# Another order of the opening steps in a fused retention and feed-forward kernel, with less VectorE work on SBUF and the last output in the score banks

## The chip, the cores and the metric

The kernel runs on one NeuronCore of a Trainium2 chip. Times are device microseconds (us) of one execution. Medians come from unchanged repeats; the profile is one of the executions. "Span" is the time from the first to the last instruction in the profile; it is about 1.7 us shorter than the device time. The engines are called PE (TensorE), DVE (VectorE), ACT (ScalarE), POOL (GpSimd) and SP (the queue that issues most loads) in profile lines.

## The reference

```python
def _attn_ref(q, k, v):                      # 8 x 8 heads x 576 x 64
    scores = (1/sqrt(64)) * (q @ k^T)
    gamma  = 1 - 2 ** (-5 - arange(H))       # one per head
    Dmat   = where(i >= j, gamma ** (i - j), 0)
    return (scores * Dmat) @ v
x   = attention, as 4608 tokens x 512
out = ((x @ w_a) * (x @ w_b)) @ w_out        # w_a, w_b 512 x 1536, w_out 1536 x 512, float32
```

The kernel does the matmuls in bf16. It never forms `Dmat`: the decay is split into a factor on each value row (`vs`) and one on each output row (`qs`), and keys outside a 128-row block come in through a running state.

## The kernel before

The feed-forward (36 block rows of 128 tokens) keeps PE busy for most of the span. It can only start once the first 512 tokens of x exist. The opening makes these in four steps, each of 256 tokens (`n`) and four heads (`hh`). All q, k, v pieces of a step (256 KB each) are loaded, cast to bf16, transposed on PE, and go through scores, state and output:

```python
STEPS = [(0, 0), (1, 0), (0, 1), (1, 1)]            # (n, hh): order 0, 1, 2, 3
for i, which in ((0, Q), (0, K), (2, K), (2, Q), (1, Q), (0, V),
                 (1, K), (1, V), (3, K), (3, Q), (2, V), (3, V)):
    load_step(*STEPS[i], which)                     # on SP's queue
...
def output_step(i):
    o = ps_o[0].tile([128, 2, 512], FP32, tag="o", name="o0")      # one buffer
    ... # matmuls: state x q, then values x masked scores
    nc.vector.tensor_tensor(x_of(...), o, qs, op=ALU.mult)         # scaled, PSUM to SBUF
...
warm(8, 512)                # dummy matmuls while nothing has landed
for c in range(HP):
    make_qs(c, 0, 512)      # four tables of decay factors, on ScalarE
cast_step(0, Q, "dve"); cast_step(0, K, "dve")
transpose_step(0, Q, "dve"); ...; transpose_step(0, K, "act")      # copies out of PSUM
warm(4, 256); score_step(0)
...                         # steps 2, 1, 3 interleaved, with dummies
state_step(3, (0,))
for F in range(3):
    ffn_begin(F)            # six of the first twelve w_a matmuls
output_step(3)
warm(3, 256)
```

`warm(count, n)` issues dummy matmuls of n columns that keep PE active. Later in the kernel, in the second half of the first feed-forward block, tiles 4 and 5 (128 tokens each) are made on the side, and then pairs of tiles. The argument will touch these lines, which the change leaves alone:

```python
def cast(i, on="pool"):                    # tiles 4 and 5: on == "dve"
    nc.scalar.copy(qb, qf)                 # q on ScalarE
    if on == "dve":
        nc.vector.tensor_copy(kb, kf)      # k on VectorE, SBUF to SBUF
...
def state(i):                              # the last of these, i == 5
    for r in (0, 1):
        rows = slice(64 * r, 64 * r + 64)
        nc.vector.tensor_copy(sums[rows, 3], kv[rows, :, rows])
        nc.scalar.copy(into[rows, 0], kv[rows, :, rows])
...
def ahead(n):                              # pairs of tiles, n = 3 first
    for w, t in ((0, qf), (1, kf)):
        nc.gpsimd.tensor_copy(qkb[0:64, w], t[0:64])     # 64 x 1024 on GpSimd
```

Of the kernel before, what the change touches and what calls it, by code (L numbers as in the profile page):

```python
# [10 lines left out]
FP32 = mybir.dt.float32  # L11
# [3 lines left out]
ALU = mybir.AluOpType  # L15
# [3 lines left out]
def kernel(  # L19
# [10 lines left out]
    nc = tc.nc  # L30

    B, H, S, D = q.shape
# [5 lines left out]
    HP = H // 2  # L38
# [24 lines left out]
    const = pool("const", 1)  # L63
# [13 lines left out]
    ps_sc = pool("ps_sc", 1, PS)  # L77
    opening, ps_o = ExitStack(), {}
# [80 lines left out]

    STEPS = [(0, 0), (1, 0), (0, 1), (1, 1)]  # L160
    Q, K, V = 0, 1, 2
    for i, which in ((0, Q), (0, K), (2, K), (2, Q), (1, Q), (0, V),
                     (1, K), (1, V), (3, K), (3, Q), (2, V), (3, V)):
        load_step(*STEPS[i], which)


# [1 line left out]
    idxp_i = const.tile([128, 6], INT32)  # L168
# [20 lines left out]
    mask3 = const.tile([128, 64], BF16)  # L189

    def make_masks():
        nc.gpsimd.iota(idxv_i, pattern=[[256, BL], [128, 2]], base=0,
                       channel_multiplier=1)
        nc.gpsimd.memset(mask, 1.0)
        nc.gpsimd.affine_select(
            out=mask, in_=mask, compare_op=ALU.is_ge, fill=0.0,
            base=0, pattern=[[1, 128]], channel_multiplier=-1)
        nc.gpsimd.tensor_copy(mask2, mask)
        nc.gpsimd.memset(mask2[0:64, 64:128], 0.0)

    ones = const.tile([128, 512], BF16)
    nc.vector.memset(ones, 1.0)  # L202
    lgp = const.tile([128, HP], FP32)
    for c in range(HP):
        nc.vector.memset(lgp[0:64, c:c + 1], math.log(gammas[2 * c]))
        nc.vector.memset(lgp[64:128, c:c + 1], math.log(gammas[2 * c + 1]))
    biasq = const.tile([128, 1], FP32)
    nc.vector.memset(biasq, math.log(scale))
    idxp_f = const.tile([128, 6], FP32)
    nc.vector.tensor_copy(idxp_f, idxp_i)  # L210
    nc.vector.tensor_scalar_add(idxp_f[64:128, 4:5], idxp_f[64:128, 4:5],
                                -float(S))
    vs = const.tile([128, H, 6], FP32)
    for h in range(H):
        nc.scalar.activation(vs[:, h, :], idxp_f, AF.Exp,
# [7 lines left out]
    def make_qs(c, s0, s1):  # L223
        nc.scalar.activation(qs[:, c, s0:s1], idx_f[:, s0:s1], AF.Exp,  # L224
                             bias=biasq[:, 0:1], scale=lgp[:, c:c + 1])
# [32 lines left out]
                                 name="state2")  # L258
    states = [two_states[:, i] for i in (0, 1)]
    state_after = const.tile([128, 2, 2, HP, 128], BF16)  # L260
    for t in (state_after, two_states):
        nc.vector.memset(t, 0.0)

    def load_w(f0, f1, which="ab"):
        if "a" in which:
            nc.gpsimd.dma_start(wa_sb[:, :, f0:f1], wa_r[:, :, f0:f1])
        if "b" in which:
            nc.gpsimd.dma_start(wb_sb[:, :, f0:f1], wb_r[:, :, f0:f1])
# [34 lines left out]
    def given(i, which):  # L303
        n, hh = STEPS[i]
        return paired[n][which][:, hh * DM:(hh + 1) * DM].rearrange(
            "p (h k d) -> p h k d", h=4, k=2)

    def by_parity(t):
        return t.rearrange("p (k h d) -> p h k d", h=4, k=2)
# [4 lines left out]
    def cast_step(i, w, on):  # L314
        COPY[on](by_parity(natural[STEPS[i]][0][:, w]), given(i, w))

    def values_step(i, kp, on):
        n, hh = STEPS[i]
        on.tensor_tensor(
            by_parity(natural[n, hh][1])[:, :, kp], given(i, 2)[:, :, kp],  # L320
            vs[:, 4 * hh:4 * hh + 4, 2 * n + kp].unsqueeze(2)
            .to_broadcast([128, 4, D]), op=ALU.mult)

    def transpose_step(i, w, on):
        qkb, qkT = natural[STEPS[i]][0], transposed[STEPS[i]]
        tp = ps_ffn.tile([128, 4, 128], BF16, tag="ab", name="tp")
        for c in range(4):
            nc.tensor.transpose(tp[:, c, :], qkb[:, w, c * 128:c * 128 + 128],  # L328
                                identity)
        COPY[on](qkT[:, w], tp.rearrange("p c x -> p (c x)"))  # L330
# [26 lines left out]
    def state_step(i, behinds):  # L357

        n, hh = STEPS[i]
        kv = ps_ffn.tile([128, 2, 2, 64], FP32, tag="ab", name="kv0")  # L360
        fresh = {0, 1}
        for behind in behinds:
            parts = [(0, slice(0, 128))] if n else []
            parts.append((n, slice(0, 128) if behind else half(0)))
            for m, rows in parts:
                qkb, vb = natural[m, hh]
                for j in (0, 1):
                    for kp in (0, 1):
                        for r in (0, 1):
                            e0 = kp * 256 + (2 * j + r) * 64  # L370
                            nc.tensor.matmul(  # L371
                                kv[half(r), behind, j, :],
                                qkb[rows, 1, e0:e0 + 64],
                                vb[rows, e0:e0 + 64],
                                start=r in fresh, stop=True,
                                skip_group_check=True)
                            fresh.discard(r)
        which = slice(behinds[0], behinds[-1] + 1)
        for r in (0, 1):
            nc.scalar.copy(  # L380
                state_after[half(r), n, which, 2 * hh:2 * hh + 2, half(r)],
                kv[half(r), which])

    def output_step(i):
        n, hh = STEPS[i]
        vb = natural[n, hh][1]
        sT = scored.pop((n, hh))
        o = ps_o[0].tile([128, 2, 512], FP32, tag="o", name="o0")
        for a in (0, 1):
            if (n, a) == (0, 0):  # L390
                continue
            st = state_after[:, 0, 0] if (n, a) == (0, 1) else (
                state_after[:, n - 1 + a, 1 - a])
            for j in (0, 1):
                nc.tensor.matmul(o[:, a, 128 * j:128 * j + 128],
                                 st[:, 2 * hh + j, :],
                                 queries((n, hh), slice(0, 128), j, a),
                                 start=(j == 0), stop=True,
                                 skip_group_check=True)
        for j in (0, 1):  # L400
            for kp in (0, 1):
                for a, r in QUADS:
                    e0 = kp * 256 + (2 * j + r) * 64
                    nc.tensor.matmul(  # L404
                        o[half(r), a, 128 * j:128 * j + 128],
                        vb[half(a), e0:e0 + 64],
                        sT[half(a), r, j, kp],
                        start=((n, a, j, kp) == (0, 0, 0, 0)), stop=True,
                        skip_group_check=True)
        cs = slice(2 * hh, 2 * hh + 2)  # L410
        nc.vector.tensor_tensor(
            x_of(256 * n, 256)[:, cs].rearrange("p j (a s) -> p a j s", a=2),
            o[:, :, 0:256].rearrange("p a (j s) -> p a j s", j=2),
            qs[:, cs, 256 * n:256 * n + 256]
            .rearrange("p j (a s) -> p a j s", a=2), op=ALU.mult)
# [416 lines left out]
    def warm(count, n):  # L832

        w = ps_ffn.tile([128, 512], FP32, tag="ab", name="w")
        for _ in range(count):
            nc.tensor.matmul(w[:, 0:n], ones[:, 0:128], ones[:, 0:n],  # L836
                             start=True, stop=True)
# [1 line left out]
    W1, W2 = 128 * WCOLS[0], 128 * (WCOLS[0] + WCOLS[1])  # L839
    vector, pool_ = nc.vector, nc.gpsimd  # L840
    warm(8, 512)
    for c in range(HP):
        make_qs(c, 0, 512)
    for i in range(4):
        place_step(i)
    cast_step(0, Q, "dve")
    cast_step(0, K, "dve")
    transpose_step(0, Q, "dve")
    cast_step(2, K, "pool")
    transpose_step(0, K, "act")  # L850
    warm(4, 256)
    score_step(0)
    transpose_step(2, K, "act")
    warm(4, 256)
    cast_step(1, Q, "act")
    cast_step(2, Q, "pool")
    transpose_step(2, Q, "act")
    warm(4, 256)
    transpose_step(1, Q, "dve")
    values_step(0, 0, pool_)  # L860
    values_step(0, 1, vector)
    warm(2, 256)
    score_step(2)
    cast_step(1, K, "act")
    state_step(0, (0, 1))
    warm(4, 256)
    transpose_step(1, K, "act")
    load_w(0, W1, "a")
    values_step(1, 0, vector)
    warm(3, 256)  # L870
    output_step(0)
    values_step(1, 1, pool_)
    load_w(0, W1, "b")
    score_step(1)
    cast_step(3, K, "act")
    state_step(1, (0,))
    transpose_step(3, K, "act")
    cast_step(3, Q, "pool")
    warm(4, 256)
    transpose_step(3, Q, "act")  # L880
    values_step(2, 0, vector)
    values_step(2, 1, pool_)
    output_step(1)
    state_step(2, (0, 1))
    score_step(3)
    values_step(3, 1, pool_)
    warm(4, 256)
    output_step(2)
    values_step(3, 0, pool_)
    load_w(W1, W2)  # L890
    state_step(3, (0,))
    for F in range(3):
        ffn_begin(F)
    output_step(3)
    warm(3, 256)
    load_w(W2, DFF)
    for i in (0, 1, 2):
        load_wo(i)
# [100 lines left out]
```

## Time and profile before

| | before |
|---|---|
| median | 334.66 us (334.39 to 335.38, 3 runs) |
| span of the profile | 332.6 us |
| PE busy | 98% of the span |
| first scores start | 7.16 us |
| first matmul with w_b starts | 21.33 us |

Two parts of the profile's page: busy time of PE, and the chain of work that ended last, as shares of the span by engine.

```profile
PE 324.5 (98%) x3616; PEld 167.5 (50%) x3616; DVE 166.0 (50%) x305; ACT 128.2 (39%) x270; POOL 113.8 (34%) x146
...
PE 94%; ACT 2%; DVE 2%; issue 1%; ACTq 0%; DVEq 0%
```

PE bounds the kernel. After 40 us it hardly waits at all; the list of waits of PE from 40 us to the end has only this (total us, times, longest):

```profile
PE o L705 <- ACT fence L733: 1.0, 3, 0.4
PE pa L772 <- DVE xT L532: 0.6, 1, 0.6
```

So the time that can be won cheaply lies in the opening. These are lines of the timeline before 24 us (start, duration, engine, source line, operation, tiles out<-in, and in brackets the engine's idle time before it and what ended it).

```profile
3.58 3.05 ACT L224 ACTIVATE qs<-qs,biasq,lgp 128x512 f32<-128x512 f32 x4
...
7.16 0.42 PE L343 MATMUL sc<-qkT 64*64 64x128 bf16 x16 [0.73 <-ACT qkT L330]
...
7.38 0.61 POOL L315 CAST qkb<-qf 128x512 bf16<-128x512 f32 x1 [0.23 <-DMA qf<-in_q_dram]
...
17.20 1.47 PE L754 MATMUL pa<-xT,wa_sb 128*128 128x512 bf16 x6
...
19.30 0.69 DVE L411 TENSOR_TENSOR xT<-o,qs 128x512 bf16<-128x512 f32 x1 [1.70 <-PE o L404]
...
20.04 1.45 PE L772 MATMUL pa<-xT,wa_sb 128*128 128x512 bf16 x6 [0.36 <-DVE xT L411]
...
21.33 1.03 PE L787 MATMUL pb<-xT,wb_sb 128*128 128x512 bf16 x4
```

ScalarE makes all four tables (3.05 us) before it copies the first transposed keys, so the first scores start at 7.16 us. GpSimd's cast of step 2's q at 7.38 us waited for its load: from there the loads come in one at a time, about 0.9 us apart. At the end, six matmuls on w_a run at 17.20 us, then the last output, then PE waits for VectorE to scale it (0.69 us) before it can go on with w_a at 20.04 us. The first w_b matmul at 21.33 us is a good mark for the whole opening: all twelve first w_a matmuls are over by then, in either order.

### The profile page before, as it was taken

What the parts mean: (1) busy time and instruction counts of PE and PEld (TensorE: products, weight loads), DVE (VectorE), ACT (ScalarE), POOL (GpSimd) and SP (SyncE); (2) the same over time, 40 slices, a digit from 0 to 9 for tenths busy, and PEclk for the clock granted to TensorE, in tenths of its full rate; (3) what the DMA queues carried; (4) which work ended last, traced back from release to release, by engine and by line L of the source; (5) the groups of instructions that cost most, each with busy time, mean ns of one, the idle gap of its engine ahead of it and who ended that gap; (6) DMA issues with size and microseconds to landing.
All of it is one profiled execution on the core that took longest, in us unless ns stands there. A gap on an engine that the chain in (4) does not pass through costs nothing.

```text
span 332.6 us, 8646 instructions
## 1 busy us (share of the span) xinstructions
PE 324.5 (98%) x3616; PEld 167.5 (50%) x3616; DVE 166.0 (50%) x305; ACT 128.2 (39%) x270; POOL 113.8 (34%) x146
## 2 busy tenths in 40 slices
PE   6999999999999999999999999999999999999996
PEld 3744446858644554545454545454545454444443
DVE  5845446456745464566247623762476347414321
ACT  7734833434515344353134323523352334213321
POOL 4780038570548468157044503470340000000000
PEclk9999999999999999999999999999999999999999
DMA  7999999999999999897599259955960420020002
GB/s 207 254 183 208 198 224 209 233 190 183 168 207 236 220 213 257 175 220 132 131 227 213 51 140 191 203 90 142 198 105 3 131 62 0 3 95 32 2 32 95
DMA packets 146151, 50.37 MB, mean 151 GB/s; under 512 B 130624, under 2 KB 141632, under 8 KB 146112
## 3 DMA queue, kind: packets, MB, share of 16 engines
q1 hardware_dynamic: 141360, 45.10, 65.0%
q0 software_dynamic: 4752, 4.72, 8.7%
q8 instruction: 28, 0.46, 0.6%
q14 instruction: 11, 0.09, 0.1%
HBM read 37.75 MB, written 9.44 MB: 142 GB/s over the span
## 4 chain that ended last, share of the span: by engine, by line
PE 94%; ACT 2%; DVE 2%; issue 1%; ACTq 0%; DVEq 0%
PE pa L772 28%; PE pb L787 28%; PE po L807 28%; PE o L692 2%; PE o L705 1%; PE sc L666 1%; PE kv L615 1%; ACT qs L224 1%; PE kv L371 1%; PE w L836 1%; PE tp L328 0%; PE o L404 0%; PE pa L754 0%; PE sc L343 0%; ACT qkT L330 0%
## 5 line engine op out<-in xcount | busy, mean ns | idle before, releaser
L792 DVE TENSOR_TENSOR hT<-ha,pb 128x512 bf16<-128x512 bf16 (+1 forms) x120 | 75.9, 634 | 97.8 <-PE pb L787 85.4
L780 ACT CAST ha<-pa 128x512 bf16<-128x512 f32 (+1 forms) x120 | 64.8, 543 | 123.1 <-PE pa L772 122.4
L787 PE MATMUL pb<-xT,wb_sb 128*128 128x512 bf16 (+1 forms) x480 | 111.8, 358 | 0.1
L772 PE MATMUL pa<-xT,wa_sb 128*128 128x512 bf16 (+1 forms) x474 | 110.3, 358 | 1.1 <-DVE xT L532 0.6
L807 PE MATMUL po<-wo_sb,hT 128*128 128x512 bf16 (+1 forms) x444 | 97.3, 374 | 0.0
L787 PEld LDWEIGHTS <-wb_sb 128*128 128x128 bf16 x480 | 46.7, 98 | 47.3 <-issue 1.1
L772 PEld LDWEIGHTS <-wa_sb 128*128 128x128 bf16 x474 | 45.3, 98 | 46.9 <-issue 2.5
L807 PEld LDWEIGHTS <-hT 128*128 128x128 bf16 x444 | 42.4, 98 | 47.0
L555 POOL CAST qkb<-qf 64x1024 bf16<-64x1024 f32 x15 | 15.5, 1030 | 86.9 <-DMA qf<-in_q_dram 82.7
L818 DVE COPY osb<-po 128x512 f32<-128x512 f32 (+1 forms) x18 | 12.2, 676 | 44.8 <-PE po L807 44.8
L560 POOL TENSOR_TENSOR vb<-vf,vs 128x1024 bf16<-128x1024 f32 x15 | 28.5, 1902 | 8.3 <-DMA vf<-in_v_dram 4.5
L816 ACT COPY osb<-po 128x512 f32<-128x512 f32 (+1 forms) x19 | 10.9, 575 | 45.3 <-PE po L807 45.3
L714 DVE TENSOR_TENSOR xT<-o,qs 128x512 bf16<-128x512 f32 x30 | 19.6, 681 | 5.5 <-PE o L705 5.5
L634 DVE TENSOR_TENSOR sums<-kv,sums 128x256 f32<-128x256 f32 x47 | 19.9, 422 | 4.6 <-PE kv L615 3.1
L675 DVE TENSOR_TENSOR sT<-sc,mask 128x512 bf16<-128x512 f32 x30 | 19.8, 680 | 0.0
L559 POOL CAST qkb<-qf 64x512 bf16<-64x512 f32 x30 | 17.8, 619 | 1.8 <-DMA qf<-in_q_dram 1.2
L559 POOL CAST qkb<-kf 64x512 bf16<-64x512 f32 x30 | 17.6, 614 | 0.9
L646 ACT CAST states<-sums 64x512 bf16<-64x512 f32 (+1 forms) x30 | 17.2, 574 | 0.5
L555 POOL CAST qkb<-kf 64x1024 bf16<-64x1024 f32 x15 | 15.5, 1035 | 5.4 <-DMA kf<-in_k_dram 4.9
L836 PE MATMUL w<-ones 128*128 128x256 bf16 (+1 forms) x40 | 8.5, 342 | 1.5 <-DVE ones L202 1.5
L431 POOL TENSOR_TENSOR vb<-vf,vs 128x512 bf16<-128x512 f32 x2 | 2.1, 1060 | 21.7 <-DMA vf<-in_v_dram 21.7
L224 ACT ACTIVATE qs<-qs,biasq,lgp 128x384 f32<-128x384 f32 (+1 forms) x12 | 8.0, 733 | 2.4 <-DVE qs L247 2.4
(103 smaller groups left out, 158.3 us busy)
## 6 DMA issues: line engine op xcount, KB each, us to landing
qf<-in_q_dram SPq DMA_DIRECT2D x32, 256.0 KB, 4.6
kf<-in_k_dram SPq DMA_DIRECT2D x32, 256.0 KB, 5.2
vf<-in_v_dram SPq DMA_DIRECT2D x32, 256.0 KB, 5.0
out_dram<-osb SPq DMA_DIRECT2D x31, 256.0 KB, 2.2
wo_sb<-in_moe_w_out_dram POOLq DMA_DIRECT2D x3, 512.0 KB, 17.0
out_dram<-osb SPq DMA_DIRECT2D x10, 128.0 KB, 2.8
qf<-in_q_dram SPq DMA_DIRECT2D x8, 128.0 KB, 4.1
kf<-in_k_dram SPq DMA_DIRECT2D x8, 128.0 KB, 5.4
```

The lines of the kernel that those rows point to most:

```text
L555: nc.gpsimd.tensor_copy(qkb[0:64, w], t[0:64])
L559: nc.gpsimd.tensor_copy(to[:, :, 1 - r], fro[:, :, r])
L560: nc.gpsimd.tensor_tensor(vb.rearrange("p (k h d) -> p k h d", k=2, h=H), vf.rearrange("p (k h d) -> p k h d", k=2, h=H), vs2[:, n % BL].u ...
L634: nc.vector.tensor_tensor(sums[:, i], own, prev, op=ALU.add)
L646: nc.scalar.copy(into[half(1 - r)].rearrange("p (k a) c d -> p a k (c d)", a=2)[:, 1, which.start // 2: which.stop // 2], sums[half(r)].re ...
L675: nc.vector.tensor_tensor(sT[:, on].rearrange("p c k s -> p (c k) s"), sc[:, on].rearrange("p c k s -> p (c k) s"), mask3.unsqueeze(1).to_ ...
L714: nc.vector.tensor_tensor(x_of(t0, 128).rearrange("p c (a s) -> p c a s", a=2), o[:, :, :, kp].rearrange("p a c s -> p c a s"), qs[:, :, s ...
L772: nc.tensor.matmul(pa[:, 0:n], wa_sb[:, c, fs], xT[:, c], start=(c == 0), stop=(c == NC - 1))
L780: nc.scalar.copy(ha[:, 0:n], pa[:, 0:n])
L787: nc.tensor.matmul(pb[:, 0:n], wb_sb[:, c, fs], xT[:, c], start=(c == 0), stop=(c == NC - 1))
L792: nc.vector.tensor_tensor(hT[:, F, 0:n], has[F][:, 0:n], pb[:, 0:n], op=ALU.mult)
L807: nc.tensor.matmul(po[:, 0:width], hT[:, F, u * 128:(u + 1) * 128], wo_sb[:, F, cols], start=(F == 0), stop=(F == NF - 1))
```

## The change

The intent, in short: do the steps in the order 0, 2, 1, 3, so that step 0's v is loaded third and states and outputs are not waited for; make only the tables that are needed first; leave VectorE the copies and products that read PSUM, and let ScalarE and GpSimd scale the values in SBUF; let GpSimd cast step 1's k before it issues the first weight load; and put the last output in the PSUM banks of the scores, so that it needn't wait for the output before it. The core of the diff:

```diff
-    for i, which in ((0, Q), (0, K), (2, K), (2, Q), (1, Q), (0, V),
-                     (1, K), (1, V), (3, K), (3, Q), (2, V), (3, V)):
+    for i, which in ((0, Q), (0, K), (0, V), (2, Q), (2, K), (1, K),
+                     (1, Q), (2, V), (3, K), (3, Q), (1, V), (3, V)):
...  (idxp_f made ahead of lgp; two_states cleared later, by GpSimd)
     def values_step(i, kp, on):
+        if on is nc.scalar:
+            for h in range(4):
+                on.mul(to[:, h], fro[:, h], by[:, h:h + 1])
...
-    def output_step(i):
+    def output_step(i, place=None):
+        else:
+            o = place.tile([128, 2, 512], FP32, tag="sc", name="o0")
...
-    for c in range(HP):
-        make_qs(c, 0, 512)
+    make_qs(0, 0, 512)
     cast_step(0, Q, "dve"); cast_step(0, K, "dve")
+    make_qs(1, 0, 512)
+    transpose_step(0, Q, "act"); transpose_step(0, K, "dve")
+    values_step(0, 0, nc.scalar); values_step(0, 1, vector)
...
+    cast_step(2, K, "pool")
+    cast_step(1, K, "pool")
...
+    load_w(0, W1, "a")
...  (step 2, then output 0, step 1, step 3; 28 dummies of 256 columns, not 32)
+    state_step(3, (0,))
+    output_step(1)
+    output_step(3, ps_sc)
     for F in range(3):
         ffn_begin(F)
-    output_step(3)
-    warm(3, 256)
```

(Short lines are joined here with semicolons.)

More of the change, by code (lines that the diff above doesn't have):

```diff
@@ L191, in make_masks @@
     def make_masks():
+        nc.gpsimd.memset(two_states, 0.0)
         nc.gpsimd.iota(idxv_i, pattern=[[256, BL], [128, 2]], base=0,
@@ L202 @@
     nc.vector.memset(ones, 1.0)
+    idxp_f = const.tile([128, 6], FP32)
+    nc.vector.tensor_copy(idxp_f, idxp_i)
+    nc.vector.tensor_scalar_add(idxp_f[64:128, 4:5], idxp_f[64:128, 4:5],
+                                -float(S))
     lgp = const.tile([128, HP], FP32)
@@ L208 @@
     nc.vector.memset(biasq, math.log(scale))
-    idxp_f = const.tile([128, 6], FP32)
-    nc.vector.tensor_copy(idxp_f, idxp_i)
-    nc.vector.tensor_scalar_add(idxp_f[64:128, 4:5], idxp_f[64:128, 4:5],
-                                -float(S))
     vs = const.tile([128, H, 6], FP32)
@@ L260 @@
     state_after = const.tile([128, 2, 2, HP, 128], BF16)
-    for t in (state_after, two_states):
-        nc.vector.memset(t, 0.0)
+    nc.vector.memset(state_after, 0.0)
     def load_w(f0, f1, which="ab"):
@@ L318, in values_step @@
         n, hh = STEPS[i]
-        on.tensor_tensor(
-            by_parity(natural[n, hh][1])[:, :, kp], given(i, 2)[:, :, kp],
-            vs[:, 4 * hh:4 * hh + 4, 2 * n + kp].unsqueeze(2)
-            .to_broadcast([128, 4, D]), op=ALU.mult)
+        to, fro = by_parity(natural[n, hh][1])[:, :, kp], given(i, 2)[:, :, kp]
+        by = vs[:, 4 * hh:4 * hh + 4, 2 * n + kp]
+        if on is nc.scalar:
+            for h in range(4):
+                on.mul(to[:, h], fro[:, h], by[:, h:h + 1])
+        else:
+            on.tensor_tensor(to, fro, by.unsqueeze(2)
+                             .to_broadcast([128, 4, D]), op=ALU.mult)
     def transpose_step(i, w, on):
@@ L387, in output_step @@
         sT = scored.pop((n, hh))
-        o = ps_o[0].tile([128, 2, 512], FP32, tag="o", name="o0")
+        if place is None:
+            o = ps_o[0].tile([128, 2, 512], FP32, tag="o", name="o0")
+        else:
+            o = place.tile([128, 2, 512], FP32, tag="sc", name="o0")
         for a in (0, 1):
@@ L847 @@
     cast_step(0, K, "dve")
-    transpose_step(0, Q, "dve")
-    cast_step(2, K, "pool")
-    transpose_step(0, K, "act")
+    make_qs(1, 0, 512)
+    transpose_step(0, Q, "act")
+    transpose_step(0, K, "dve")
+    values_step(0, 0, nc.scalar)
+    values_step(0, 1, vector)
+    make_qs(2, 0, 512)
+    cast_step(2, Q, "pool")
     warm(4, 256)
     score_step(0)
-    transpose_step(2, K, "act")
+    warm(3, 256)
+    state_step(0, (0, 1))
+    warm(1, 256)
+    transpose_step(2, Q, "dve")
+    cast_step(2, K, "pool")
+    cast_step(1, K, "pool")
     warm(4, 256)
+    transpose_step(2, K, "dve")
+    warm(4, 256)
+    load_w(0, W1, "a")
     cast_step(1, Q, "act")
-    cast_step(2, Q, "pool")
-    transpose_step(2, Q, "act")
-    warm(4, 256)
-    transpose_step(1, Q, "dve")
-    values_step(0, 0, pool_)
-    values_step(0, 1, vector)
-    warm(2, 256)
     score_step(2)
-    cast_step(1, K, "act")
-    state_step(0, (0, 1))
-    warm(4, 256)
     transpose_step(1, K, "act")
-    load_w(0, W1, "a")
-    values_step(1, 0, vector)
-    warm(3, 256)
     output_step(0)
-    values_step(1, 1, pool_)
+    transpose_step(1, Q, "act")
+    values_step(2, 1, pool_)
+    values_step(2, 0, pool_)
+    make_qs(3, 0, 512)
     load_w(0, W1, "b")
+    warm(5, 256)
     score_step(1)
-    cast_step(3, K, "act")
-    state_step(1, (0,))
-    transpose_step(3, K, "act")
-    cast_step(3, Q, "pool")
+    warm(1, 256)
+    cast_step(3, Q, "act")
+    state_step(2, (0, 1))
+    cast_step(3, K, "pool")
     warm(4, 256)
     transpose_step(3, Q, "act")
-    values_step(2, 0, vector)
-    values_step(2, 1, pool_)
-    output_step(1)
-    state_step(2, (0, 1))
-    score_step(3)
-    values_step(3, 1, pool_)
-    warm(4, 256)
-    output_step(2)
-    values_step(3, 0, pool_)
-    load_w(W1, W2)
-    state_step(3, (0,))
+    transpose_step(3, K, "dve")
+    output_step(2)
+    for kp in (0, 1):
+        values_step(1, kp, pool_)
+    values_step(3, 0, nc.scalar)
+    values_step(3, 1, pool_)
+    load_w(W1, W2)
+    score_step(3)
+    state_step(1, (0,))
+    warm(2, 256)
+    state_step(3, (0,))
+    output_step(1)
+    output_step(3, ps_sc)
     for F in range(3):
         ffn_begin(F)
-    output_step(3)
-    warm(3, 256)
     load_w(W2, DFF)
```

## The prediction

> **What bounds the kernel now.** TensorE: busy 324.5 of 332.6 us (page, busy times); the chain that ended last is 94% PE. The list of waits from 40 us on gives PE 1.6 us of idle. The change touches the opening only. The timeline of 0 to 24 us shows what limits it:
> - Loads: 256 KB pieces of q, k and v land about 0.9 us apart from 6.4 us on, the twelfth at 14.5 us. GpSimd waited 3.0 us for step 2's k and 1.3 us for a v.
> - ScalarE: the first keys' copy waits behind four table activations (3.05 us, to 6.6 us), so the first scores start at 7.16 us.
> - The end: six first matmuls (17.20 us) run before the last output; the next six wait for its scaling (VectorE, 0.69 us) until 20.04 us. The first matmul with w_b starts at 21.33 us.
>
> **What the change does.** TensorE's work stays, except 28 instead of 32 dummy matmuls of 256 columns.
> - Two of the four tables (0.76 us each) leave the path to the first scores, and a 0.48 us memset leaves VectorE ahead of the first casts (4.85 us). I estimate the first scores at 6.1 us, now limited by the eight dummies that end at 5.0 us.
> - v of step 0 takes the third load slot, so its state is ready before 9 us.
> - VectorE loses its value scalings except the first (0.42 us each; one took 0.58 us beside GpSimd); ScalarE takes two as four products each (estimated 0.8 us together). The Trainium skill ("GPSIMD Engine Reference", Specifications) says both engines share SBUF interfaces; 0.58 against 0.42 us agrees, but that is 0.16 us.
> - GpSimd casts step 1's k, then issues the first weight DMA at 9.8 us, as before (9.84 us). It landed 7.3 us after issue: at 17.1 us again, just in time. The second weight DMA moves from 11.6 to 12.1 us and is needed at 20.3 us.
> - The last output sits in the score banks and needn't wait for the previous output's scaling: the last two outputs run back to back, and the first twelve feed-forward matmuls without a wait.
>
> **Estimate.** I laid out both kernels' instructions by engine order, with the trace's durations and landing times. For before this puts the second six matmuls at 20.02 us (traced: 20.04). For after, the first six start at 17.7 us, the next at 19.0, w_b's at 20.3: 1.0 us earlier than 21.33. All of it is on the chain, which is PE from there on. Later data keep about 1 us of slack or more: the second group of w_a columns lands at 22.5 us and is needed at 23.9 (before 24.88).
>
> **Predicted: 333.7 us, range 333.0 to 334.6** (0.3% faster). Faster by over 2%: 0.005; within 2%: 0.99; slower by over 2%: 0.005.
>
> **What would show it.** First scores near 6.1 us; last output's scaling over before 18.5 us, not 20.0; no PE wait within the first twelve feed-forward matmuls; w_b's first matmul near 20.3 us. From there a constant offset to the old trace, with PE idle after 40 us still about 1.6 us.
>
> **What would make it wrong.** The first weights landing after 17.7 us, or w_b's after 20.3, since they share the DMA engines with v; v of step 1, now eleventh, landing late; VectorE copies queued behind a 1.22 us mask; a granted clock below 1.0; the gain lost at a later wait, such as that for tile 5's scaling (0.55 us at 55.2 us).

## The result

| | before | changed |
|---|---|---|
| median | 334.62 us (334.39 to 335.38, 4 runs) | 334.14 us (333.96 to 334.36, 4 runs) |
| ratio | | 0.9982, 95% interval 0.9965 to 0.9999 |
| span of the profile | 332.6 us | 332.6 us |

The ratio is the mean time of the one kernel's fast runs over that of the other's of the same rounds, so it is not quite the ratio of the medians. About 0.5 us was gained, where 0.9 us had been predicted (333.7 against 334.62), and the two profiled executions, both at a granted clock of 1.000, have the same span. Busy times and chain after the change:

```profile
PE 324.9 (98%) x3612; PEld 167.4 (50%) x3612; DVE 166.8 (50%) x304; ACT 128.7 (39%) x275; POOL 115.3 (35%) x148
...
PE 93%; DVE 2%; DMA 2%; ACT 1%; issue 1%; SPq 0%; POOL 0%; ACTq 0%; DVEq 0%; POOLq 0%
```

The timeline of the opening, changed kernel:

```profile
6.20 0.42 PE L347 MATMUL sc<-qkT 64*64 64x128 bf16 x16
...
7.64 0.61 POOL L315 CAST qkb<-qf 128x512 bf16<-128x512 f32 x1 [3.87 <-DMA qf<-in_q_dram]
...
17.42 1.37 DVE L418 TENSOR_TENSOR xT<-o,qs 128x512 bf16<-128x512 f32 x2 [0.56 <-PE o L411]
...
18.16 1.46 PE L761 MATMUL pa<-xT,wa_sb 128*128 128x512 bf16 x6
...
19.45 1.46 PE L779 MATMUL pa<-xT,wa_sb 128*128 128x512 bf16 x6
...
20.75 1.03 PE L794 MATMUL pb<-xT,wb_sb 128*128 128x512 bf16 x4
```

The opening is what was intended: first scores 0.96 us earlier, the two last outputs scaled back to back, twelve w_a matmuls in a row. The first w_b matmul comes at 20.75 us, 0.58 us earlier than before. Yet the span is the same. The list of waits of PE from 40 us on tells where this went:

```profile
PE o L712 <- ACT fence L740: 1.0, 3, 0.4
PE tp L452 <- DVE qkb L435: 0.6, 1, 0.6
PE pa L779 <- DVE xT L539: 0.6, 1, 0.6
```

The first and third were there before. The second is new: a transpose waits 0.56 us for a cast on VectorE, that of tile 5's k. The timeline around it, first of the kernel before, then of the changed one:

```profile
48.92 1.03 POOL L555 CAST qkb<-qf 64x1024 bf16<-64x1024 f32 x1 [1.45 <-DMA qf<-in_q_dram]
...
49.87 0.42 DVE L428 CAST qkb<-kf 128x512 bf16<-128x512 f32 x1
...
49.99 1.32 POOL L559 CAST qkb<-qf 64x512 bf16<-64x512 f32 x2
```

```profile
48.97 1.03 POOL L562 CAST qkb<-qf 64x1024 bf16<-64x1024 f32 x1 [1.43 <-DMA qf<-in_q_dram]
...
49.28 0.99 DVE L435 CAST qkb<-kf 128x512 bf16<-128x512 f32 x1
...
50.04 1.27 POOL L566 CAST qkb<-qf 64x512 bf16<-64x512 f32 x2
...
50.34 0.40 PE L452 MATMUL tp<-identity,qkb 128*128 128x128 bf16 x4 [0.56 <-DVE qkb L435]
```

GpSimd's first cast for pair 3 starts when its load lands, at 48.9 us in both. VectorE's k cast follows PE. Before, it came at 49.87 us, just as GpSimd's cast ended (48.92 + 1.03 = 49.95), and took 0.42 us. Now that PE is earlier, it comes at 49.28 us, in the middle of GpSimd's cast, and takes 0.99 us: it ends 0.27 us after GpSimd's (50.27 against 50.00). From there on the two traces agree to a few hundredths (second token block at 55.22 us in both).

### The profile page after: what moved, and what is told of

It reads as the page before. It is cut to its first block, busy times and chain, and to the rows that moved or that the text cites. A ratio compares the mean times of both kernels' runs of the same rounds, so it can differ in the third digit from the quotient of the medians.

```text
span 332.6 us, 8648 instructions
## 1 busy us (share of the span) xinstructions
PE 324.9 (98%) x3612; PEld 167.4 (50%) x3612; DVE 166.8 (50%) x304; ACT 128.7 (39%) x275; POOL 115.3 (35%) x148
## 4 chain that ended last, share of the span: by engine, by line
PE 93%; DVE 2%; DMA 2%; ACT 1%; issue 1%; SPq 0%; POOL 0%; ACTq 0%; DVEq 0%; POOLq 0%
PE pb L794 28%; PE pa L779 28%; PE po L814 27%; DMA qf<-in_q_dram 2%; PE o L699 2%; PE o L712 1%; PE sc L673 1%; PE kv L622 1%; PE kv L375 1%; PE tp L332 1%; PE w L843 0%; SPq L154 0%; PE pa L761 0%; DVE xT L539 0%; PE sc L347 0%
```

## The experiments

**Theories.** H (held cast): the opening gains about 0.6 us, and where the k cast meets GpSimd's cast, the gain is given back, because VectorE is held off until the running GpSimd instruction ends. L (loads): the gain is lost since later tiles are bound by their loads. S (sharing): VectorE and GpSimd only slow each other down while both are busy. For the opening: either it is limited by PE, or by the landing of loads.

### e1: the changed kernel again

No edit.

> The changed kernel as it is, as a control. Theory H (held cast): the opening gains 0.58 us, and tile 5's k cast on VectorE, which meets GpSimd's first pair cast, gives most of it back: 0.3 to 0.5 us faster than before, with a PE wait of about 0.5 us ahead of tile 5's second transposes near 50.3 us in the profile. Theory L (loads): the gain is lost because the tiles' loads bind; same time, but the wait is put down to a load.

Measured: 334.24 us median (333.67 to 335.87, 6 runs) against 334.45 for before, ratio 0.9996 (0.9976 to 1.0017): in these rounds no gain is clear of the noise. The profiled execution was the fastest, 333.67 us, and it did not show the expected wait: w_b's first matmul at 20.48 us, and the k cast ran ahead of GpSimd's, not into it.

```profile
49.01 0.41 DVE L435 CAST qkb<-kf 128x512 bf16<-128x512 f32 x1
...
49.30 1.03 POOL L562 CAST qkb<-qf 64x1024 bf16<-64x1024 f32 x1 [1.43 <-PE po L814]
```

Here the opening's gain reached the second token block whole (54.37 us against 55.22). So the collision is a matter of a few tenths in the timing of one execution. Two executions of one kernel, one with the collision and one without, already speak for H and against L. The stretch from the first w_b matmul to the second token block says the same: 33.89 us in the kernel before and in this trace, 34.47 us in the changed kernel's first trace, with the collision.

### e2: tile 5's k cast on ScalarE

```diff
     def cast(i, on="pool"):
-        if on == "dve":
+        if i == 5:
+            nc.scalar.copy(kb, kf)
+        elif on == "dve":
             nc.vector.tensor_copy(kb, kf)
```

> The changed kernel with tile 5's k cast on ScalarE instead of VectorE. Theory H: the wait near 50.3 us goes, first matmul of the second token block at about 54.7 us instead of 55.2, and the time falls by about 0.4 to 0.55 us against the changed kernel: 333.6 to 333.7 us, 0.9 to 1.0 us faster than before. Theory L: no change, the transposes still wait.

Measured: 333.45 us (333.25 to 333.64, 6 runs), ratio 0.9966 (0.9952 to 0.9980): 1.0 us faster than before, as H expected. The wait is gone, and the second token block starts at 54.06 us. The six runs lie within 0.4 us, those of e1 in the same rounds within 2.2 us; that is not shown to be the cast's doing, since the first four runs of the changed kernel also lay within 0.4 us, and those of e7 and e9 below, with the same move, within 1.7 and 4.3 us. Its opening, in the timeline:

```profile
6.76 0.42 PE L347 MATMUL sc<-qkT 64*64 64x128 bf16 x16
...
7.07 0.61 POOL L315 CAST qkb<-qf 128x512 bf16<-128x512 f32 x1 [3.30 <-DMA qf<-in_q_dram]
...
20.33 1.03 PE L796 MATMUL pb<-xT,wb_sb 128*128 128x512 bf16 x4
```

The first scores are later than in the changed kernel's first trace (6.76 against 6.20 us) and yet w_b comes earlier (20.33 against 20.75). What was earlier is the load of step 2's q. This is taken up below.

### e3: the same move in the kernel before

The edit of e2, applied to the kernel before.

> The kernel before with the same move of tile 5's k cast. Theory H: no change (within 0.15 us), since there the cast took its usual 0.42 us between two GpSimd casts and PE hardly waited. Rival: the move is good in itself, whatever the opening; then this too is 0.4 us or more faster than before.

Measured: 334.40 us (334.13 to 334.59, 6 runs) against 334.45, ratio 0.9993 (0.9980 to 1.0006): no change that the times can show. The traces show a small one: from the first w_b matmul to the second token block it is 33.74 us here (33.73 in e2), against 33.89 in the kernel before. So the move is worth 0.15 us in either opening, and the rest of its gain only behind the new one. With e2 this settles that the collision, and not the loads of L, took the gain: it was there, and one cast on another engine gives it back. Whether VectorE is held to the end, as H says, or slowed, as S says, is for e11 and e12.

### e4: GpSimd's first pair cast cut in two

```diff
     def ahead(n):
         for w, t in ((0, qf), (1, kf)):
-            nc.gpsimd.tensor_copy(qkb[0:64, w], t[0:64])
+            for part in ((slice(0, DM), slice(DM, 2 * DM))
+                         if (n, w) == (3, 0) else (slice(0, 2 * DM),)):
+                nc.gpsimd.tensor_copy(qkb[0:64, w, part], t[0:64, part])
```

> The changed kernel with GpSimd's first cast for pair 3 cut in two halves of 512 columns (0.55 us each instead of 1.03). If a GpSimd instruction holds VectorE's two-port cast off until that instruction ends, the k cast lasts about 0.4 to 0.55 us instead of 0.99 and the transposes go on about 0.45 us earlier: 0.3 to 0.45 us faster than the changed kernel. If instead the two share the bandwidth for as long as GpSimd is busy, the cast still lasts about 1 us and nothing changes.

Measured: 334.61 us (333.68 to 336.12, 6 runs), ratio 1.0008 (0.9984 to 1.0031), so the expected gain did not come. It is no test of the hold either: in the profiled execution the opening was late (w_b at 21.05 us), the first half was cast at 47.98 us, and the k cast came at 49.59 us, when the second half (49.08 to 49.69 us) was as good as over. Inconclusive; e11 and e12 make the meeting certain.

### e11 and e12: GpSimd kept busy on purpose

```diff
     def cast(i, on="pool"):          # of the changed kernel
         natural[i] = (qkb, qb, kb, vb)
+        if i == 5:
+            for _ in range(4):                                        # e11
+                nc.gpsimd.tensor_copy(idle[0:64], qs[0:64, 0:2, 0:512])
+            for _ in range(30):                                       # e12, instead
+                nc.gpsimd.tensor_copy(idle[0:64, 0, 0:32], qs[0:64, 0, 0:32])
```

> The changed kernel with four needless GpSimd casts of 64x1024 (about 1.03 us each) put in from about 47.5 us on, so that VectorE's k cast of tile 5 (0.42 us alone) surely meets one. If VectorE is held off until the running GpSimd instruction ends, the cast ends 0.2 to 0.35 us after the end of the GpSimd cast in which it began (or it begins at a boundary and takes 0.42). If the two share, its end has no tie to those ends and it takes 0.6 to 1.0 us.

> The same with thirty GpSimd casts of 64x32 (about 0.1 us each) over about the same time. If the hold lasts to the end of one instruction, the k cast takes 0.42 to 0.6 us although GpSimd is busy all the time. If busy GpSimd slows VectorE by sharing, 0.6 to 1.0 us as with the long ones.

Single looks, state unknown; only the cast is read from them. First e11 (timeline from 49.5 us), then e12 (from 49.2 us):

```profile
49.40 2.21 POOL L446 CAST idle<-qs 64x1024 bf16<-64x1024 f32 x2
...
49.72 0.99 DVE L435 CAST qkb<-kf 128x512 bf16<-128x512 f32 x1
```

```profile
49.10 0.64 POOL L446 CAST idle<-qs 64x32 bf16<-64x32 f32 x2
...
49.26 0.42 DVE L435 CAST qkb<-kf 128x512 bf16<-128x512 f32 x1
```

In e11 the k cast began 0.32 us into a GpSimd cast of 1.03 us (49.40 to 50.43 us) and ended 0.28 us after it. In the changed kernel that was 0.31 us in and 0.27 us after. In e12, with GpSimd issuing one short cast every 0.27 us, the k cast took its 0.42 us; it was GpSimd that stretched, two short casts taking 0.64 us. These two do not yet rule out S. In e11 the k cast met the GpSimd cast at the same place as in the changed kernel's first trace (0.32 and 0.31 us in), so a VectorE that is only slowed would end at the same place too; and in e12 the short casts left GpSimd idle a part of the time (they took 0.20 us of each 0.27 us). The kept traces of the changed opening settle it, with another pair of instructions. Near 24 us VectorE casts a small table (`idxv`, 0.17 us alone) while GpSimd fills another (`idx_i`, 0.61 us). In the changed kernel and in e4:

```profile
23.75 0.61 POOL L244 IOTA idx_i<- 128x576 int32 x1
...
23.83 0.56 DVE L236 CAST idxv<-idxv_i 128x18 f32<-128x18 int32 x1
```

```profile
23.85 0.61 POOL L244 IOTA idx_i<- 128x576 int32 x1
...
24.13 0.36 DVE L236 CAST idxv<-idxv_i 128x18 f32<-128x18 int32 x1
```

In eight traces (the changed kernel, e1, e2, e4, e5, e9, e11, e12) the cast starts while the 0.61 us instruction runs, at places from 0.01 to 0.46 us into it, and takes 0.18 to 0.63 us; it ends 0.03 us after GpSimd's end in all eight. An end that stays while the start moves fits H and not S. In the other direction, GpSimd's instruction that starts during a VectorE cast takes longer too: in the first traces of both kernels, e4, e11 and e12 it loses 0.08 to 0.17 us, always 0.14 us less than the time that the cast still had to run. So the one that comes second waits for the one that runs, in both directions.

The Trainium skill says in "GPSIMD Engine Reference", section "Specifications", that GpSimd's SBUF interfaces are shared with VectorE, with contention for VectorE instructions in a two-port mode or with two SBUF inputs; and in "VectorE: DVE Perf Modes", section "Mode 2×_2P — use both read ports for one tensor", that a one-source operation from SBUF to SBUF can use both read ports, which a PSUM source cannot. The traces agree: in the changed kernel the copies from PSUM keep their 0.42 us beside a GpSimd cast, as at 8.74 us here:

```profile
8.51 0.61 POOL L315 CAST qkb<-kf 128x512 bf16<-128x512 f32 x1 [0.26 <-DMA kf<-in_k_dram]
...
8.74 0.42 DVE L334 COPY qkT<-tp 128x512 bf16<-128x512 bf16 x1 [0.75 <-PE tp L332]
```

### e10: two value scalings back on VectorE

```diff
 # on e2
-    values_step(2, 0, pool_)
+    values_step(2, 0, vector)
-    for kp in (0, 1):
-        values_step(1, kp, pool_)
+    values_step(1, 0, vector)
+    values_step(1, 1, pool_)
```

> The changed kernel with the cast's move (e2), and one of the value scalings of step 2 and one of step 1 back on VectorE. If keeping VectorE on PSUM matters in the opening, step 1's scaling there stands behind step 2's output scaling and is held off by GpSimd beside it, step 1's state comes 0.5 to 0.8 us later, and the time is 0.4 to 0.8 us more than e2's 1.0 us under before. If it doesn't matter, the same as e2.

Measured: 334.11 us (333.82 to 334.30, 6 runs), ratio 0.9980 (0.9963 to 0.9998), which is 0.0014 of 334.5 us, or 0.5 us, worse than e2's ratio. That ratio is of another set of rounds, and the two intervals overlap. The trace says more clearly that something was lost: w_b comes 13.79 us after the cast of step 2's q, against 13.02 to 13.33 us without this edit (table below). It has the expected wait:

```profile
15.58 0.41 DVE L325 TENSOR_TENSOR vb<-vf,vs 128x256 bf16<-128x256 f32 x1
...
16.05 0.31 PE L375 MATMUL kv<-vb,qkb 64*64 64x64 bf16 x8 [0.50 <-DVE vb L325]
```

Step 1's state waits for a scaling that stood behind VectorE's output scaling of step 2 (14.97 to 15.66 us). It was not held by GpSimd there (0.41 us): what hurts in this place is VectorE's queue. The other scaling, that of step 2, did lose time beside GpSimd: it took 0.69 us instead of 0.42, at 12.07 us, while GpSimd issued a weight DMA and then began a cast. How the loss divides between the two was not tested.

### e5 and e6: an attempt at the last wait

The last PE wait of 0.55 us, at the start of the second token block, is for tile 5's scaling, which stands behind four state copies that take turns on VectorE and ScalarE. Both kernels below have the edit of e2 and put the copies off; e5 has the new opening, e6 the old.

```diff
     def state(i):                    # i == 5
-            for r in (0, 1):
-                nc.vector.tensor_copy(sums[rows, 3], kv[rows, :, rows])
-                nc.scalar.copy(into[rows, 0], kv[rows, :, rows])
+            late.append(copies)      # copies: the same four (def left out here), run at place 150
+    todo += [(150, lambda: late.pop()(), ())]
```

> The changed kernel with tile 5's k cast on ScalarE, and the copies of tile 5's running state (two on VectorE, two on ScalarE, taking turns) put off until after tile 5's output scaling. If PE's wait of 0.55 us at the start of the second token block is only that the scaling stands behind those copies on VectorE, the wait goes: 332.9 to 333.1 us, 0.5 us less than with the cast's move alone (333.45), 1.4 to 1.6 us less than before. Rival: PE then waits elsewhere (for the state copies, or a busy output bank), and under 0.2 us is gained.

> The kernel before with both of these moves and the old opening. It has the old opening's 0.6 to 1.0 us more than e5 and nothing else: 333.7 to 333.9 us. This gives the worth of the opening with no collision after it: e6 minus e5, 0.6 to 1.0 us.

Measured: e5 334.44 us, e6 334.85 us, before 335.29 us in these rounds (334.27 to 335.97, 11 runs). e5's profiled run, and it alone, was slow (343.03 us at a granted clock of 0.959) and is left out; the median changes by nothing. Both expectations of time were missed. The wait went, but another came, here in e6:

```profile
58.06 0.37 ACT L481 CAST states<-kv 64x256 bf16<-64x256 f32 x1 [0.49 <-DVE sums L480]
58.45 0.37 ACT L784 CAST ha<-pa 128x256 bf16<-128x256 f32 x1
...
58.88 0.60 PE L791 MATMUL pb<-xT,wb_sb 128*128 128x256 bf16 x4 [1.03 <-ACT ha L784]
```

ScalarE's state copy waits for VectorE's, and the feed-forward's eviction of `pa` stands behind it in ScalarE's queue. PE loses 1.03 us where it had lost 0.55. The difference of the two is the opening's worth with no collision after it: 0.4 us by the medians, but 0.8 us by the ratios (0.9973 and 0.9996, where one run of e6 took 336.92 us). So these times do not decide whether it is the 0.6 to 1.0 us expected.

### e7: six dummies fewer

```diff
 # on e5
     score_step(1)
-    warm(1, 256)
     cast_step(3, Q, "act")
...
-    warm(4, 256)
+    warm(1, 256)
     transpose_step(3, Q, "act")
...
     state_step(1, (0,))
-    warm(2, 256)
     state_step(3, (0,))
```

> e5 with six of the 28 dummy matmuls of 256 columns taken away, those late in the opening (one before the last q cast, three of four before step 3's transposes, two before step 3's state). If the changed opening is limited by PE itself in those places, the first w_b matmul comes 0.2 to 0.35 us earlier and the time falls as much. If it is limited by the loads and casts of steps 1 and 3, PE only waits where the dummies stood: under 0.1 us. Granted clock stays 1.0.

Measured: 334.12 us (333.29 to 334.99, 6 runs) against e5's 334.44, ratio 0.9968 (0.9950 to 0.9985) against 0.9973. That is 0.2 us by the ratios and 0.3 us by the medians, inside the intervals. The trace says more: w_b's first matmul at 20.44 us, 12.76 us after the start of the cast of step 2's q (12.79 us in e9 below, which has the same dummies), where the six traces of the unthinned opening have 13.02 to 13.33 us (table below). The dummies cost about 0.3 us there, so PE was at least in part the limit where they stood. The profile's mean clock was 0.998.

### e8: the last output back in its own bank

```diff
 # on e5
-    output_step(3, ps_sc)
+    output_step(3)
```

> e5 with the last output back in its own output bank instead of the score banks. It then waits for step 1's output to be scaled (VectorE 0.69 us): I expect the two outputs 0.6 to 0.7 us apart from each other, w_b's first matmul 0.6 to 0.75 us later, and the time up by as much, so about nothing left of the opening's gain over e6.

Measured: 334.50 us (334.35 to 335.11, 5 runs), against e5's 334.44: not the expected difference. In the trace the wait is there, and w_b comes 13.69 us after that cast, about 0.56 us more than the mean of the table:

```profile
17.72 0.38 PE L402 MATMUL o<-qkT,state_after 128*128 128x128 bf16 x4 [0.80 <-DVE xT L418]
```

So the score banks are worth about half a microsecond in the opening by the traces. The times of these rounds do not show it; their scatter (before: 1.7 us) can hide such a difference, so what it is worth in time stays open.

### e9: both moves and the thinner opening

The edit of e2, the dummies of e7, and the state copies left in place but not by turns:

```diff
-            for r in (0, 1):
-                rows = slice(64 * r, 64 * r + 64)
-                nc.vector.tensor_copy(sums[rows, 3], kv[rows, :, rows])
-                nc.scalar.copy(into[rows, 0], kv[rows, :, rows])
+            for copy, to in ((nc.vector.tensor_copy, sums[:, 3]),
+                             (nc.scalar.copy, into[:, 0])):
+                for r in (0, 1):
+                    rows = slice(64 * r, 64 * r + 64)
+                    copy(to[rows], kv[rows, :, rows])
```

> The changed kernel with tile 5's k cast on ScalarE, tile 5's two VectorE state copies ahead of its two ScalarE ones instead of by turns (so the scaling no longer stands behind a ScalarE copy, and ScalarE's copies are over before the next block), and six late dummies of the opening taken away. Expected: PE's 0.55 us wait at the start of the second token block falls under 0.15 us with no new wait near 58 us; w_b's first matmul 12.9 us after step 2's q has landed; 1.6 to 1.9 us faster than before, 0.6 to 0.9 us faster than with the cast's move alone. If putting the copies off had failed for another reason than ScalarE's copy holding up its queue, a wait of about 1 us comes back near 58 us.

Measured: 332.86 us median against 334.49 for before, 1.6 us less, as expected. Five runs lie between 332.35 and 333.70 us; the sixth took 336.66 us (before had one of 336.36 us in the same rounds), and with it the ratio is 0.9968 (0.9928 to 1.0007), so the interval does not exclude 1. Span 331.2 us. In the list of waits of PE from 40 us on, one line is left:

```profile
PE o L715 <- ACT fence L743: 1.0, 3, 0.4
```

VectorE makes its two copies in a row (52.18 us), scales tile 5 at 53.05 us, and the second block starts at 53.80 us, against 55.22 before. This is the fastest version by its median, though its rounds were not those of e2 (333.45 us).

### What limits the new opening

| trace | first scores | cast of step 2's q starts | first w_b matmul | cast to w_b |
|---|---|---|---|---|
| before, e3, e6 (old opening) | 7.16, 7.16, 7.20 | 7.38, 7.47, 7.63 | 21.33, 21.36, 21.38 | (13.75 to 13.95) |
| e2 | 6.76 | 7.07 | 20.33 | 13.26 |
| e1 | 6.14 | 7.15 | 20.48 | 13.33 |
| changed, first trace | 6.20 | 7.64 | 20.75 | 13.11 |
| e12 | 6.44 | 7.69 | 20.72 | 13.03 |
| e4 | 6.76 | 8.03 | 21.05 | 13.02 |
| e11 | 6.68 | 8.16 | 21.18 | 13.02 |

The lower six traces have one and the same opening. Their cast of step 2's q, which waits for its load in each, varies by 1.1 us, and the first w_b matmul follows it. It does not follow the first scores: e2 and e4 have them at the same time and differ by 0.72 us at the end. The old opening stayed at 21.33 to 21.38 us when its load came up to 0.25 us later. The first scores of the new opening vary with something else. "TensorE: Matmul & The Clock Gate" of the Trainium skill, Part 1, says that the window of the TensorE clock runs freely, so that the number of slow matmuls differs from run to run. The traces agree: the four dummies of 256 columns before the first scores took 0.27 us each in the changed kernel's first trace, whose record of the full clock starts at 5.22 us, and 0.42 us each in e2, whose record starts at 6.80 us. The end of the opening did not follow this. On average the new opening ends at 20.75 us, 0.6 us before the old (21.36), and between 0.2 and 1.0 us in single executions. This is read from traces that happened to differ; no experiment moved that load alone.

## Why the prediction was right or wrong

- **Class and time: right.** 334.14 us lies in the range, and the change is within 2%. The size was about twice the gain measured (0.9 predicted, 0.5 measured).
- **First scores near 6.1 us: right (6.20), but worth nothing by itself.** Traces with 6.76 us ended as early or earlier.
- **No wait within the first twelve w_a matmuls: right.** Outputs of steps 1 and 3 ran back to back as told, and undoing the bank brings a wait of 0.80 us (e8).
- **First weights just in time: right in kind.** They were not waited for.
- **"w_b's at 20.3: 1.0 us earlier": too large.** The mean of six traces is 20.75 us. Two terms were mis-sized. The prediction took the landing times of the old trace, where the cast of step 2's q started at 7.38 us; on average it started at 7.62 us. From 7.38 us to the predicted 20.3 us its layout thus has 12.9 us for the chain from there, and 13.1 us were measured. One duration in that layout was low: four products on ScalarE were put at 0.8 us and took 1.06 us; whether all of this lay on the chain was not tested.
- **"From there a constant offset to the old trace, with PE idle after 40 us still about 1.6 us": wrong, and the step that failed.** The slack of later data was checked, and it held (no PE wait is listed between 5 and 40 us). What was not checked was which engine's work an earlier PE would run into. In the first trace the offset of 0.58 us lasted until 49.4 us and then went into a new wait of 0.56 us, since VectorE's k cast met a GpSimd cast that starts when a load lands. The contention itself was known to the prediction, but was dismissed as "0.16 us" from one case in the opening. That case was itself a hold: the trace before has the scaling of 0.58 us from 11.34 us on, beside a GpSimd product from 11.03 to 11.64 us, and it ended 0.28 us after the product. In e3 and e6, with the same opening, it took 0.63 us and ended as long after. The size is not a property of the operation: it follows from what is left of the GpSimd instruction at that moment. A k cast that starts with a GpSimd cast of 1.03 us would lose about 0.9 us (an estimate: 1.03 + 0.28 - 0.42).
- **"lost at a later wait, such as that for tile 5's scaling": the right neighbourhood, the wrong wait.** The loss came at tile 5's k cast, 5 us earlier.
- **"VectorE loses its value scalings" for the sake of SBUF:** undoing two of these moves (e10) costs about 0.5 us by ratios of different rounds, and in the trace at least in part by VectorE's queue.

Shown: that a VectorE cast is held until the running GpSimd instruction ends (the first trace, e11, and the eight traces of the small cast), and that moving the k cast makes the changed kernel 0.8 us faster by the medians and leaves the time of the kernel before as it is (e1, e2, e3). Of these 0.8 us the traces account for 0.58 us by the collision (34.47 against 33.89 us from w_b to the second block) and 0.15 us by the move itself (33.74). Still open: how many of e1's six runs had the collision, since only one has a trace. Open too: single runs of 1.5 to 2 us more, which the kernel before has as well; why the fourth load lands up to a microsecond earlier or later (casts at 7.07 to 8.16 us); and what the order of the loads, GpSimd's cast of step 1's k and the later tables are worth each by itself, as none of these was undone alone. The last output's place and the value scalings were undone one at a time (e8, e10), and their worth is read from traces rather than times.

## What to carry to other kernels

When an opening gets shorter, everything tied to PE moves with it, and everything tied to loads stays: look in the trace for pairs of engines that only just missed each other, above all a VectorE instruction on SBUF beside a GpSimd instruction, because the later one waits for the whole rest of the earlier one. Put a cast that PE will wait for on ScalarE (0.61 us beside a running GpSimd cast in e3, as alone), or keep GpSimd's instructions short there. And take several traces of an opening that is fed by loads: one trace gives one draw of their landing times.

## What the Trainium skill lacked or had wrong

- "SBUF — State Buffer", "Who interferes with whom": I found no figure there, or on another page, for how long a VectorE instruction still runs once the GpSimd instruction that held it has ended. Here it is 0.28 us for a cast of 128x512 and for a product of 128x256 (0.42 us each alone), and 0.03 us for a cast of 128x18 (0.17 us alone).
- "DMA: Bandwidth & Descriptors": I found nothing there on how much the time of one and the same load differs from run to run. Here the fourth load's cast started between 7.07 and 8.16 us in six traces of one opening, and the time of the opening followed it.
